# Transposing two bf16 channels as one 4-byte element on VectorE, with TensorE reading the result at a step of 2

## The chip, the cores and the metric

One core of a Trainium2 chip (trn2). The metric is the device time of one execution in microseconds. The four runs of the kernel before agree within 0.2% of their median (244.49 to 245.45 us). All times compared here are of runs taken in the same rounds on the same chip as runs of the kernel before. Times of the profiler's span (243.1 us for the kernel before) are about 1.8 us shorter than the timed ones.

## The reference

Attention in chunks of 64 positions, then a feed-forward with a product of two branches and no other nonlinearity:

```python
# q, k, v: (8, 8, 576, 64) = batch, heads, positions, channels; chunk = 64
scores = q_c @ k_c.T / sqrt(64)              # within each chunk
attn   = softmax(scores)
x      = (attn @ v_c), heads side by side    # (4608, 512)
a, b   = x @ w1, x @ w2                      # 512 -> 1024
out    = ((a * b) @ w3) @ w_out              # 1024 -> 1024 -> 512
```

## The kernel before

The kernel works in bf16 with float32 accumulation. 4608 tokens are handled as 18 pairs of 256 tokens (p = 0 to 17). One string lists every step in program order: `T` transposes q or k, `S` scores, `E` exponential, `P` the product with v, `N` normalises, `X` transposes x, `A`, `B` the products by w1, w2, `C`, `M` make a*b, `V`, `W`, `Z` multiply w3 by w_out once, `O` the output. Lower-case letters are loads.

The kernel transposes on VectorE in blocks of 32 by 32 elements (BL = 32) and arranges channels in such blocks. For pairs 0 to 7 it uses the blocks where they lie; for later pairs a DMA moves blocks between partitions. These are the parts that the change touches (KO = 4, BL = 32, NB = 4, GT = 512, PT = 256, UT = 128, H = 8, CH = 64, FO = 8):

```python
def do_T(p, s, h=None):                  # transpose q (s=0) or k (s=1) of a pair
    g = p // 2
    if g not in qkT_t:
        qkT_t[g] = asb.tile([P, 2, 2, 2, H, CH], bf, tag="qkT", bufs=2, name="qkT")
    inorder(nc.vector.transpose(
        qkT_t[g][:, :, p % 2, s, heads(h)].rearrange("p e h (y t) -> p h t e y", t=2),
        qk_t[p][:, s, heads(h)].rearrange("p h (t e y) -> p h t e y", t=2, e=2)))

# do_S, pairs 0 to 7: two products per block, accumulated
mm(s_t[p][half[i % 2], i // 2, h * CH:(h + 1) * CH],
   lhsT=qkT_t[g][blk[i], e, m, 1, h, :], rhs=qkT_t[g][blk[i], e, m, 0, h, :],
   start=(e == 0), stop=(e == 1))

def do_X(p, u):                          # transpose x
    g, m = divmod(p, 2)
    if p < 8:
        t0 = m * PT + u * UT
        inorder(nc.vector.transpose(
            new_xt(g)[:].rearrange("p (o t) -> p o t", o=KO)[:, :, t0:t0 + UT]
            .rearrange("p o (m y) -> p m o y", y=BL),
            xn_t[p][:, u].rearrange("p r (c n) (z o) -> p (r c) o n z", c=2, o=KO)))
    else: ...                            # the same into xm, which a DMA moves into xt

# do_AB: x is the moving operand of every product by w1 and w2
rhs = new_xt(p // 2)[:].rearrange("p (o t) -> p o t", o=KO)          # p >= 8: "p (s o t) -> p o s t"
for ki in range(KO):
    mm(ps_t[p, j][:, which, i * n:(i + 1) * n],
       lhsT=(w1, w2)[which][:, ki, f * P:(f + 1) * P], rhs=rhs[:, ki],
       start=(ki == 0), stop=(ki == KO - 1))

def do_V(f):                             # transpose a part of w3
    w3T_t[f] = msb.tile([P, FO, P], bf, tag="w3T", bufs=4, name="w3T")
    inorder(nc.vector.transpose(
        w3T_t[f][:].rearrange("p k (f y) -> p f k y", y=BL),
        w3[:, NB * f:NB * (f + 1), :].rearrange("p f (k x) -> p f k x", x=BL)))
```

Products are 256 columns wide for pairs 0 to 3 (256 of them) and 512 wide from pair 4 on (448 of them).

The softmax here doesn't subtract the row's maximum and nothing guards it: scores larger than these inputs give would overflow.

## Time and profile before

| | kernel before |
|---|---|
| time, median | 244.97 us (4 runs, 244.49 to 245.45) |
| span of the profiled run | 243.1 us |
| TensorE busy | 225.9 us, 93% |
| VectorE busy | 153.7 us, 63% |
| TensorE's waits | 7.3 us for the first q, k transposes, then none over 1.4 us |

The page gives each engine's busy time, TensorE's waits by releaser, groups of instructions by line and shape, and the chain of work that ended last. In the chain of waits, "PE ab_ps x64" with its duration is 64 products by w1 and w2. The lines themselves are shown in the prediction.

### The profile page before, as it was taken

What the parts mean: (1) busy time and instruction counts of PE and PEld (TensorE: products, weight loads), DVE (VectorE), ACT (ScalarE), POOL (GpSimd) and SP (SyncE); (2) the same over time, 40 slices, a digit from 0 to 9 for tenths busy, and PEclk for the clock granted to TensorE, in tenths of its full rate; (3) what the DMA queues carried; (4) which work ended last, traced back from release to release, by engine and by line L of the source; (5) the groups of instructions that cost most, each with busy time, mean ns of one, the idle gap of its engine ahead of it and who ended that gap; (6) DMA issues with size and microseconds to landing.
All of it is one profiled execution on the core that took longest, in us unless ns stands there. A gap on an engine that the chain in (4) does not pass through costs nothing.

```text
span 243.1 us, 6347 instructions
## 1 busy us (share of the span) xinstructions
PE 225.9 (93%) x2731; PEld 120.3 (49%) x2753; DVE 153.7 (63%) x232; ACT 85.1 (35%) x116; POOL 83.3 (34%) x112
## 2 busy tenths in 40 slices
PE   1299989999999979999999999999999999999994
PEld 1247868864545444444444444444444444444443
DVE  1856799689899578999998899918440332143000
ACT  2412323423333343534326335162332332332322
POOL 8847974665986444773260240000000000000000
PEclk9999999999999999999999999999999999999999
DMA  7999999999999999999999893735502200400244
GB/s 179 179 185 180 186 168 199 196 193 170 154 172 218 226 228 252 173 219 192 209 237 213 251 137 83 173 89 203 145 0 89 86 0 0 175 0 1 86 173 173
DMA packets 93595, 37.63 MB, mean 155 GB/s; under 512 B 75008, under 2 KB 86528, under 8 KB 93568
## 3 DMA queue, kind: packets, MB, share of 16 engines
q0 software_dynamic: 82592, 18.88, 83.9%
q1 hardware_dynamic: 9936, 17.83, 24.8%
q10 hardware_dynamic: 1040, 0.52, 0.8%
q8 instruction: 21, 0.34, 0.6%
q14 instruction: 6, 0.05, 0.1%
HBM read 38.80 MB, written 9.44 MB: 198 GB/s over the span
## 4 chain that ended last, share of the span: by engine, by line
PE 70%; DMA 16%; DVE 5%; SPq 3%; issue 2%; POOL 2%; ACT 0%; DVEq 0%; POOLq 0%
PE ab_ps L92 38%; PE o_ps L92 23%; PE w_ps L92 6%; DMA w<-in_moe_w_dram 4%; DMA qkm<-qkT 3%; DMA xt<-xm 3%; DMA qk<-in_k_dram 3%; DMA qk<-in_q_dram 3%; SPq L189 3%; PE s_ps L92 2%; PE pv L92 2%; DVE qkT L197 2%; DVE xn L260 1%; DVE ab L341 1%; POOL vbuf L95 1%
## 5 line engine op out<-in xcount | busy, mean ns | idle before, releaser
L92 PE MATMUL ab_ps<-xt,w 128*128 128x512 bf16 (+1 forms) x681 | 126.8, 342 | 1.4 <-DVE xt L272 0.9
L92 PEld LDWEIGHTS <-w 128*128 128x128 bf16 x704 | 67.3, 98 | 55.4 <-DVE xt L272 1.4
L341 DVE TENSOR_TENSOR ab<-a_sb,ab_ps 128x512 bf16<-128x512 f32 x71 | 47.8, 674 | 43.5 <-ACT a_sb L326 43.3
L326 ACT COPY a_sb<-ab_ps 128x512 f32<-128x512 f32 x71 | 41.6, 586 | 81.3 <-PE ab_ps L92 81.1
L92 PE MATMUL o_ps<-w3o,ab 128*128 128x512 bf16 (+1 forms) x285 | 63.3, 373 | 0.6
L197 DVE STREAM_TRANSPOSE qkT<-qk 128x1024 bf16<-128x1024 bf16 x36 | 45.1, 1289 | 8.0 <-ACT qk L140 5.5
L92 PEld LDWEIGHTS <-ab 128*128 128x128 bf16 x296 | 28.5, 98 | 32.3
L95 POOL DMA_DIRECT2D vbuf<-in_v_dram x40 | 33.9, 855 | 17.9 <-DMA qk<-in_k_dram 4.8
L371 ACT COPY o_sb<-o_ps 128x1024 f32<-128x1024 f32 x17 | 17.2, 1012 | 45.2 <-PE o_ps L92 41.3
L260 DVE TENSOR_TENSOR xn<-pv,rc 128x512 bf16<-128x512 f32 x36 | 24.9, 692 | 1.4
L95 POOL DMA_DIRECT2D qk<-in_q_dram x23 | 18.1, 790 | 9.9 <-DMA qk<-in_k_dram 3.1
L95 POOL DMA_DIRECT2D qk<-in_k_dram x23 | 18.0, 785 | 8.8 <-DMA vbuf<-in_v_dram 5.1
L230 ACT ACTIVATE e<-s_ps 128x1024 bf16<-128x1024 f32 x16 | 15.9, 1028 | 2.5 <-PE s_ps L92 2.2
L92 PE MATMUL w_ps<-wo,w3T 128*128 128x512 bf16 x62 | 13.9, 379 | 0.1
L280 DVE STREAM_TRANSPOSE xm<-xn 128x512 bf16<-128x512 bf16 x20 | 13.6, 697 | 0.2
L257 DVE RECIPROCAL rc<-pv 128x8 f32<-128x8 f32 x36 | 6.9, 192 | 9.9 <-PE pv L92 9.9
L95 POOL DMA_DIRECT2D w<-in_moe_w_dram x16 | 11.1, 697 | 5.8 <-DMA vbuf<-in_v_dram 2.3
L92 PEld LDWEIGHTS <-e 64*32 64x32 bf16 (+1 forms) x832 | 7.8, 97 | 8.5 <-issue 7.1
L272 DVE STREAM_TRANSPOSE xt<-xn 128x512 bf16<-128x512 bf16 x16 | 11.4, 711 | 0.5
L92 PE MATMUL pv<-vbuf,e 64*32 64x65 bf16 (+1 forms) x832 | 10.2, 198 | 1.5 <-ACT e L230 1.1
L92 PEld LDWEIGHTS <-qkT 32*64 32x64 bf16 x512 | 5.5, 117 | 11.0 <-DVE qkT L197 7.9
L364 DVE COPY o_sb<-o_ps 128x256 f32<-128x256 f32 x1 | 0.4, 425 | 16.0 <-PE o_ps L92 16.0
(24 smaller groups left out, 52.9 us busy)
## 6 DMA issues: line engine op xcount, KB each, us to landing
out_dram<-o_sb SPq DMA_DIRECT2D x17, 512.0 KB, 3.2
qkm<-qkT SPq DMA_DIRECT2D x40, 128.0 KB, 4.6
vbuf<-in_v_dram POOLq DMA_DIRECT2D x32, 128.0 KB, 8.6
w<-in_moe_w_dram POOLq DMA_DIRECT2D x16, 256.0 KB, 9.6
qk<-in_q_dram POOLq DMA_DIRECT2D x11, 256.0 KB, 6.9
qk<-in_k_dram POOLq DMA_DIRECT2D x11, 256.0 KB, 7.5
xt<-xm SPq DMA_DIRECT2D x40, 64.0 KB, 3.2
wo<-in_moe_w_out_dram POOLq DMA_DIRECT2D x4, 256.0 KB, 8.4
```

The costliest lines, as they stand in the source:

```text
L92: return inorder(nc.tensor.matmul(*a, **kw))
L95: return inorder(nc.gpsimd.dma_start(dst, src))
L189: inorder(nc.sync.dma_start(dst, src))
L197: inorder(nc.vector.transpose(qkT_t[g][:, :, p % 2, s, heads(h)].rearrange("p e h (y t) -> p h t e y", t=2), qk_t[p][:, s, heads(h)].rearr ...
L230: inorder(nc.scalar.activation(e_t[p][:, :, heads(hh)], s_t[p][:].rearrange("p u (h q) -> p u h q", q=CH)[:, :, heads(hh)], Exp, scale=sca ...
L257: inorder(nc.vector.reciprocal(rc[:], pv[:, :, :, D:W]))
L260: inorder(nc.vector.tensor_mul(xn_t[p][:, u], pv[:, :, :, 0:D], rc.to_broadcast([P, 2, 4, D])))
L272: inorder(nc.vector.transpose(new_xt(g)[:].rearrange("p (o t) -> p o t", o=KO)[:, :, t0:t0 + UT] .rearrange("p o (m y) -> p m o y", y=BL), ...
L280: inorder(nc.vector.transpose(xm_t[g][:, u, :, m].rearrange("p o (c y) -> p c o y", y=BL), xn_t[p][:].rearrange("p u r m d -> p (u r) m d" ...
L326: inorder(nc.scalar.copy(a_t[p, j][:], ps_t[p, j][:, 0, :]))
L341: inorder(nc.vector.tensor_mul(o, view(a_t.pop((p, j))[:]), view(ps_t.pop((p, j))[:, 1, :])))
L371: inorder(nc.scalar.copy(o_sb[:], ps_t.pop(p)[:]))
```

## The change

In the profile before, a transpose of 512 elements per partition takes 697 ns and one of 1024 takes 1217 ns, so each further element costs about 1.02 ns. The intent is to halve the elements: two neighbouring bf16 channels are transposed as one 4-byte element. The result has the two channels interleaved, so that TensorE must read one channel at a step of two elements. This is done for q and k of pairs 0 to 7, for x of all pairs, and for w3.

```diff
 # do_T
-            qkT_t[g] = asb.tile([P, 2, 2, 2, H, CH], bf, ...)
+            qkT_t[g] = asb.tile([P, 2, 2, 2, H, CH] if p >= 8 else [P, 2, 2, H, CH, 2], bf, ...)
+        if p < 8:
+            inorder(nc.vector.transpose(
+                qkT_t[g][:, p % 2, s, heads(h)].rearrange("p h y e -> p h (y e)").bitcast(f32)
+                .rearrange("p h (y t) -> p h t y", t=2),
+                qk_t[p][:, s, heads(h)].bitcast(f32).rearrange("p h (t y) -> p h t y", t=2)))
+            return
 # do_S
-   lhsT=qkT_t[g][blk[i], e, m, 1, h, :], rhs=qkT_t[g][blk[i], e, m, 0, h, :],
+   lhsT=qkT_t[g][blk[i], m, 1, h, :, e], rhs=qkT_t[g][blk[i], m, 0, h, :, e],
 # do_X (the branch for p >= 8 likewise)
-                new_xt(g)[:].rearrange("p (o t) -> p o t", o=KO)[:, :, t0:t0 + UT]
+                new_xt(g)[:].bitcast(f32).rearrange("p (o t) -> p o t", o=KO // 2)[:, :, t0:t0 + UT]
                 .rearrange("p o (m y) -> p m o y", y=BL),
-                xn_t[p][:, u].rearrange("p r (c n) (z o) -> p (r c) o n z", c=2, o=KO)))
+                xn_t[p][:, u].bitcast(f32).rearrange("p r (c n) (z o) -> p (r c) o n z", c=2, o=KO // 2)))
 # do_AB
-            rhs = new_xt(p // 2)[:].rearrange("p (s o t) -> p o s t", s=2, o=KO)
+            rhs = new_xt(p // 2)[:].rearrange("p (s a t b) -> p a b s t", s=2, a=KO // 2, b=2)
-            rhs = new_xt(p // 2)[:].rearrange("p (o t) -> p o t", o=KO)
+            rhs = new_xt(p // 2)[:].rearrange("p (a t b) -> p a b t", a=KO // 2, b=2)
-                   lhsT=(w1, w2)[which][:, ki, f * P:(f + 1) * P], rhs=rhs[:, ki],
+                   lhsT=(w1, w2)[which][:, ki, f * P:(f + 1) * P], rhs=rhs[:, ki // 2, ki % 2],
 # do_V, do_W: w3T becomes [P, FO // 2, P, 2], written as f32, read as lhsT=w3T[:, ki // 2, :, ki % 2]
 # load_wo: rows of w_out in the matching order, two at a time (half the packets)
 # ... cut
```

More of the change, by code (lines that the diff above doesn't have):

```diff
@@ L177, in load_wo @@
         for i in range(NB):
-            load(wo[i * BL:(i + 1) * BL],
-                 moe_w_out[i * DF // NB:(i + 1) * DF // NB].rearrange("(k x) n -> x k n", x=BL))
+            load(wo[i * BL:(i + 1) * BL].rearrange("p (k e) n -> p k (e n)", e=2),
+                 moe_w_out[i * DF // NB:(i + 1) * DF // NB].rearrange("(k x e) n -> x k (e n)", x=BL, e=2))
     half = [slice(0, CH), slice(CH, P)]
@@ L195, in do_T @@
         if g not in qkT_t:
-            qkT_t[g] = asb.tile([P, 2, 2, 2, H, CH], bf, tag="qkT", bufs=2, name="qkT")
+            qkT_t[g] = asb.tile([P, 2, 2, 2, H, CH] if p >= 8 else [P, 2, 2, H, CH, 2], bf,
+                                tag="qkT", bufs=2, name="qkT")
+        if p < 8:
[4 more added lines that the diff above has]
+            return
         inorder(nc.vector.transpose(
@@ L272, in do_X @@
             inorder(nc.vector.transpose(
-                new_xt(g)[:].rearrange("p (o t) -> p o t", o=KO)[:, :, t0:t0 + UT]
+                new_xt(g)[:].bitcast(f32).rearrange("p (o t) -> p o t", o=KO // 2)[:, :, t0:t0 + UT]
                 .rearrange("p o (m y) -> p m o y", y=BL),
-                xn_t[p][:, u].rearrange("p r (c n) (z o) -> p (r c) o n z", c=2, o=KO)))
+                xn_t[p][:, u].bitcast(f32).rearrange("p r (c n) (z o) -> p (r c) o n z", c=2, o=KO // 2)))
         else:
             if g not in xm_t:
-                xm_t[g] = asb.tile([P, 2, KO, 2, UT], bf, tag="xm", bufs=2, name="xm")
+                xm_t[g] = asb.tile([P, 2, KO // 2, 2, 2 * UT], bf, tag="xm", bufs=2, name="xm")
             inorder(nc.vector.transpose(
-                xm_t[g][:, u, :, m].rearrange("p o (c y) -> p c o y", y=BL),
-                xn_t[p][:].rearrange("p u r m d -> p (u r) m d")[:, :, 2 * u:2 * u + 2]
-                .rearrange("p c n (z o) -> p c o n z", o=KO)))
+                xm_t[g][:, u, :, m].bitcast(f32).rearrange("p o (c y) -> p c o y", y=BL),
+                xn_t[p][:].bitcast(f32).rearrange("p u r m d -> p (u r) m d")[:, :, 2 * u:2 * u + 2]
+                .rearrange("p c n (z o) -> p c o n z", o=KO // 2)))
     def do_H(g, a):
@@ L303, in do_AB @@
         if p >= 8:
-            rhs = new_xt(p // 2)[:].rearrange("p (s o t) -> p o s t", s=2, o=KO)
+            rhs = new_xt(p // 2)[:].rearrange("p (s a t b) -> p a b s t", s=2, a=KO // 2, b=2)
         else:
-            rhs = new_xt(p // 2)[:].rearrange("p (o t) -> p o t", o=KO)
+            rhs = new_xt(p // 2)[:].rearrange("p (a t b) -> p a b t", a=KO // 2, b=2)
             if p < 4:
-                rhs = rhs[:, :, p % 2 * PT:(p % 2 + 1) * PT]
+                rhs = rhs[:, :, :, p % 2 * PT:(p % 2 + 1) * PT]
         fs = (f,) if p >= 4 else (2 * j, 2 * j + 1)
@@ L380, in do_V @@
     def do_V(f):
-        w3T_t[f] = msb.tile([P, FO, P], bf, tag="w3T", bufs=4, name="w3T")
+        w3T_t[f] = msb.tile([P, FO // 2, P, 2], bf, tag="w3T", bufs=4, name="w3T")
         inorder(nc.vector.transpose(
-            w3T_t[f][:].rearrange("p k (f y) -> p f k y", y=BL),
-            w3[:, NB * f:NB * (f + 1), :].rearrange("p f (k x) -> p f k x", x=BL)))
+            w3T_t[f][:].rearrange("p k y e -> p k (y e)").bitcast(f32).rearrange("p k (f y) -> p f k y", y=BL),
+            w3[:, NB * f:NB * (f + 1), :].bitcast(f32).rearrange("p f (k x) -> p f k x", x=BL)))
     def do_W(m):
@@ L390, in do_W @@
             for ki in range(FO):
-                mm(ps_t["w", m][:, i, :], lhsT=w3T[:, ki, :], rhs=wo[:, ki, :],
+                mm(ps_t["w", m][:, i, :], lhsT=w3T[:, ki // 2, :, ki % 2], rhs=wo[:, ki, :],
                    start=(ki == 0), stop=(ki == FO - 1))
```

## The prediction

> **What bounds the kernel now.** I read the busy times first, then TensorE's waits, then the busy times by stretch, the groups by shape, and last the timeline and the chain of waits over the first 40 us.
>
> The page's busy line, the summary of TensorE's waits, and one run of products from the chain of waits:
>
> ```profile
> PE 225.9 (93%) x2731; PEld 120.3 (49%) x2753; DVE 153.7 (63%) x232; ACT 85.1 (35%) x116; POOL 83.3 (34%) x112
> ...
> PE z_ps L92 <- DVE qkT L197: 7.3, 1, 7.3
> PE s_ps L92 <- issue: 1.4, 1, 1.4
> PE z_ps L92 <- DVE zero L110: 1.2, 1, 1.2
> PE pv L92 <- ACT e L230: 1.1, 1, 1.1
> PE ab_ps L92 <- DVE xt L272: 0.9, 2, 0.6
> ...
> 208.78 13.81 PE ab_ps L92 x64
> ```
>
> TensorE is busy for 225.9 of 243.1 us. A busy TensorE need not be at its peak, so I checked the rate: 13.81 us for 64 products of 512 columns is 215.8 ns each. Its work counted up: 448 + 64 + 280 products of 512 columns (x by w1 and w2 from pair 4 on; w3 by w_out; the output) at 215.8 ns make 170.9 us, 256 of 256 columns at 114.7 ns (32 in 3.67 us on the timeline) make 29.4, the last output's 16 half-wide ones about 1.8, scores and PV of 18 pairs at about 0.65 us each some 23.5. That is 225.6, so nearly all of the busy time is work at full rate. Only the idle 17.2 us can be won without making TensorE's work itself cheaper, and this change does not. Of that, 3.2 us lie after the last product, 1.2 before the first; the waits above show where the rest is. VectorE is the cause of two entries, 7.3 and 0.9 us.
>
> Busy times by stretch show that VectorE's load elsewhere costs nothing:
>
> ```profile
> 50.00:60.00 10.00, 9.95 (x56) 5.34 (x55) 10.00 (x11) 3.20 (x4) 5.63 (x8) 1.00 1.81 181
> 120.00:130.00 10.00, 9.95 (x77) 4.73 (x78) 9.90 (x15) 3.79 (x5) 3.69 (x5) 1.00 1.26 219
> ```
>
> Columns after the width: TensorE, weight load, VectorE, ScalarE, GpSimd. VectorE is full in both stretches and TensorE is busy for 9.95 of 10 us all the same: the order is tuned so that VectorE works ahead.
>
> The groups by shape, for the sizes (busy us, mean ns):
>
> ```profile
> L197 DVE STREAM_TRANSPOSE qkT<-qk 128x1024 bf16<-128x1024 bf16 x36 | 45.1, 1289 | 8.0 <-ACT qk L140 5.5 <-DMA qk<-in_q_dram 1.3 <-PE s_ps L92 0.9
> L280 DVE STREAM_TRANSPOSE xm<-xn 128x512 bf16<-128x512 bf16 x20 | 13.6, 697 | 0.2
> L272 DVE STREAM_TRANSPOSE xt<-xn 128x512 bf16<-128x512 bf16 x16 | 11.4, 711 | 0.5
> L382 DVE STREAM_TRANSPOSE w3T<-w 128x1024 bf16<-128x1024 bf16 x8 | 9.4, 1217 | 1.7 <-DMA w<-in_moe_w_dram 1.7
> ```
>
> 512 and 1024 elements take 697 and 1217 ns: 520/512 = 1.016 ns per element and 177 ns fixed.
>
> The two places where VectorE delays TensorE, on the timeline, and the piece of the chain of waits before the second:
>
> ```profile
> 5.93 1.99 ACT L140 CAST qk<-raw 128x1024 bf16<-128x1024 f32 x2 [3.39 <-DMA raw<-in_q_dram]
> 7.00 5.33 DVE L197 STREAM_TRANSPOSE qkT<-qk 128x1024 bf16<-128x1024 bf16 x4 [5.46 <-ACT qk L140]
> 9.54 1.07 PE L92 MATMUL z_ps<-qkT 32*64 32x64 bf16 x64 [7.31 <-DVE qkT L197]
> ...
> 24.09 3.67 PE L92 MATMUL ab_ps<-xt,w 128*128 128x256 bf16 x32 [0.33 <-DVE xt L272]
> ...
> 35.48 1.92 PE L92 MATMUL ab_ps<-xt,w 128*128 128x256 bf16 x16 [0.55 <-DVE xt L272]
> ...
> 23.61 6.76 DMA qk<-in_q_dram
> 30.38 0.02 issue
> 30.40 1.32 DVE qkT L197
> ```
>
> The first scores wait for two transposes in a row. The product at 35.48 us waits for a chain that starts with q of pair 3 landing at 30.38: one q transpose, one product ab, then twice (rc, xn, xt).
>
> [...] The changed q, k transpose writes 4-byte elements at a step of two words[...]. The trace speaks neither way: in the x transpose each bf16 read is 8 bytes from the last and still runs at 697 to 711 ns, but that is a read. [...] No operand of TensorE in the kernel before has a step[...]. [...]
>
> **The change part by part.** The order of instructions is the same on every engine; only shapes change.
>
> 1. q, k of pairs 0 to 7: 16 transposes from 1024 bf16 to 512 4-byte elements. 177 + 512 x 1.016 = 697, plus about 40 for the stepped write (1289 against 1217 before shows 72 for twice the elements): about 740 ns instead of 1289. 16 x 0.55 = 8.8 us off VectorE.
> 2. x: 36 transposes from 512 to 256 elements, 177 + 260 = about 437 instead of 697 to 711. 36 x 0.265 = 9.5 us off.
> 3. w3: 8 from 1217 to about 697, 4.2 us off.
> 4. w_out lands in rows twice as long: half the packets for 1 MB, a small relief for the DMA.
> 5. TensorE: the same products, moving x at a step of 2, scores with both operands at a step of 2, w3's weights at a step of 2. I take 0 for this.
>
> So VectorE falls by 22.5 us, from 153.7 to about 131. On the path that sets the end there is far less. At the start: the second cast ends at 7.92 us, so the second transpose ends near 8.7, not 9.5, and the first scores start about 0.8 us earlier. The following wait is unchanged, since the exponential follows the scores. But this gain is provisional: weights arrive in step with the DMA (99% busy from the second slice to the 24th), and products up to 35 us cannot run ahead of them. The chain that ends at 35.48 is fixed at its start by the landing at 30.38. It shortens by one q transpose (1.32 to 0.74: 0.58) and two x transposes (0.27 each: 0.54), in all 1.1 us, so X's end moves from 35.43 to about 34.3. TensorE, which was ready at 34.93, would be ready at about 34.0 to 34.5 with the earlier gain partly stopped by weights. So the product at 35.48 starts near 34.4: 1.1 us won. From there to the end TensorE runs almost without a wait, and the 1.1 us is carried; I take 0.1 off for waits that reappear. 245.2 - 1.0 = 244.2 us.
>
> **The rivals.** (a) The stepped read slows TensorE. Then the loss is large: if each 512-wide product took 1.1 times as long, 448 x 21.6 ns = 9.7 us, and if twice, 97 us and more. If only the scores' weight loads took twice as long, 8 pairs x up to 0.6 us, some 4 us. For it: nothing in the trace has such a read. [...] I give 15% to a loss over 2%. (b) The q, k transpose doesn't reach 740 ns because of its stepped write[...]. 35% likely, and hardly visible in the time. (c) The gain is absorbed: the DMA is full until 140 us, and TensorE may meet a load that it now outruns. For it: q of pair 3 and w3's first half (VectorE waits 1.7 us for it at 49.6). Against: the first product by w3 starts at 51.7, with the transpose done at 50.9, and would now be done at 50.3. This gives 245.0. (d) The wait named issue (1.4 us in the scores at 87 us), for which the profile shows no releaser, goes or comes again elsewhere: 1.4 us either way. (e) VectorE was the bound of the middle and 10 us come free: excluded by TensorE's 9.95 of 10 us in its fullest stretches.
>
> **Range and chances.** Free steps give 243.0 to 245.3, with (d) 246. 8 in 10: 242.8 to 246.0. Over 2% faster means under 240.3, and would need 5 us of idle time where VectorE causes 8.2, most of it the start's loads and casts: 3%. Within 2%: 82%. Slower by over 2%: 15%, all of it (a).
>
> **What would show it.** Right: VectorE's busy time near 131 us, TensorE's still near 226; the x transposes at 437 ns, w3's at 697, q and k at 740[...]; the first scores at 8.7 us; the wait for xt in front of the third pair's products at 34.3 to 34.5 us; 64 products by w1, w2 still in 13.8 us. Wrong: 64 products in 15 us or more, or 64 scores in over 0.7 us (rival a); a new TensorE wait on a DMA (rival c); 4-byte transposes as long as before, with which the time would not change at all.

The forecast's sum: 245.2 us (the profiled run), less the 1.1 of the start, plus the 0.1 for waits that reappear, 244.2 us. What stands for the 4-byte transposes is an estimate from the 1.016 ns per element of bf16, and the 0 for the stepped reads was the author's estimate; the trace before had neither such a transpose nor such a read. "Full rate" is 215.8 ns per product of 512 columns.

## The result, and the profile after

| | before | after |
|---|---|---|
| time, median | 244.97 us (244.49 to 245.45) | 248.66 us (248.28 to 249.66) |
| ratio | | 1.0157 (95%: 1.012 to 1.0194) |
| span of the profiled run | 243.1 | 247.9 |
| TensorE busy | 225.9 | 230.7 |
| VectorE busy | 153.7 | 132.5 |

A ratio here is always the mean time of one kernel's runs over that of the other's of the same rounds, so not quite the ratio of the medians beside it. The change made the kernel 1.6% slower. The profiled run is the slowest of the four (249.66 us), so its spans overstate the loss by about 1 us; durations of single instructions don't suffer from this.

The busy line and the summary of TensorE's waits, after:

```profile
PE 230.7 (93%) x2731; PEld 118.9 (48%) x2753; DVE 132.5 (53%) x232; ACT 85.1 (34%) x116; POOL 83.2 (34%) x112
...
PE z_ps L92 <- DVE qkT L201: 6.7, 1, 6.7
PE ab_ps L92 <- DMA w<-in_moe_w_dram: 1.3, 2, 0.9
PE s_ps L92 <- issue: 1.2, 1, 1.2
```

VectorE lost 21 us of work, as intended. TensorE gained 4.8 us of busy time with the same instructions (its products by w1 and w2 alone gained 5.5, from 126.8 to 132.3 us on the two pages). So the loss is not a wait: TensorE itself has become slower. The groups by shape show that the transposes did what they were meant to do (busy us, mean ns):

```profile
L201 DVE STREAM_TRANSPOSE qkT<-qk 128x512 f32<-128x512 f32 x16 | 10.9, 697 | 10.8 <-ACT qk L140 5.9 <-DMA qk<-in_q_dram 3.7 <-DMA qk<-in_k_dram 1.2
L290 DVE STREAM_TRANSPOSE xm<-xn 128x256 f32<-128x256 f32 x20 | 8.2, 431 | 0.2
L282 DVE STREAM_TRANSPOSE xt<-xn 128x256 f32<-128x256 f32 x16 | 7.1, 445 | 0.5
L392 DVE STREAM_TRANSPOSE w3T<-w 128x512 f32<-128x512 f32 x8 | 5.7, 707 | 4.4 <-PE w_ps L92 2.3 <-DMA w<-in_moe_w_dram 2.0
```

The last lines of the chain of waits (start us, us, what) show where the time came from:

```profile
191.41 14.50 PE ab_ps L92 x64
...
206.18 6.64 PE o_ps L92 x30
212.82 14.50 PE ab_ps L92 x64
```

64 products by w1 and w2 took 13.81 us before and take 14.50 us now: 226.6 ns each in place of 215.8. The output products between them, which read nothing at a step, still take 6.64 us for 30. The other engines do the same work in this stretch as before (VectorE 4.8 us, ScalarE 5.1, and the DMA moves about 40 GB/s in both), so heavier traffic of theirs is not the reason. The trace's start-to-start times say the same of every stage: 226 to 227 ns at 512 columns wherever x is read, 113.3 in place of 109.2 at 256 columns, and under 1 ns between the even and the odd channel. 448 x 10.8 ns = 4.84 us, and 256 x 4.1 ns = 1.05 us, 5.9 in all. On the two timelines the wide products begin 0.1 us late (82.94 against 82.82) and have ended 4.7 us late (227.16 against 222.43): 4.6 us, and the wait named "issue" among them is 0.2 us shorter than before, so the 4.8 us are there.

The timeline of the first 40 us shows what became of the gain there (TensorE alone):

```profile
26.70 0.71 PE L92 MATMUL s_ps<-qkT 32*64 32x64 bf16 x64
27.81 1.08 PE L92 MATMUL ab_ps<-xt,w 128*128 128x256 bf16 x8 [0.40 <-DMA w<-in_moe_w_dram]
29.80 1.08 PE L92 MATMUL ab_ps<-xt,w 128*128 128x256 bf16 x8 [0.91 <-DMA w<-in_moe_w_dram]
30.81 0.70 PE L92 MATMUL pv<-vbuf,e 64*32 64x65 bf16 x64
31.44 5.62 PE L92 MATMUL ab_ps<-xt,w 128*128 128x256 bf16 x48
```

The first scores started at 8.90 us (9.54 before) and the scores above at 26.70 (27.68 before). Then TensorE had outrun the last quarter of w1 and w2, and waited for it. Behind that wait, 48 products run without a break, where before the third pair's had waited 0.55 us for x. The first product by w3 starts at 51.81 us, 51.70 before: nothing was left of the gain.

### The profile page after: what moved, and what is told of

Same layout as the page of the kernel before. It is cut to its first block, busy times and chain, and to the rows that moved or that the text cites. A ratio compares the mean times of both kernels' runs of the same rounds, so it can differ in the third digit from the quotient of the medians.

```text
span 247.9 us, 6347 instructions
## 1 busy us (share of the span) xinstructions
PE 230.7 (93%) x2731; PEld 118.9 (48%) x2753; DVE 132.5 (53%) x232; ACT 85.1 (34%) x116; POOL 83.2 (34%) x112
## 4 chain that ended last, share of the span: by engine, by line
PE 82%; DMA 11%; SPq 2%; issue 2%; POOL 1%; ACT 1%; DVE 0%; DVEq 0%; POOLq 0%
PE ab_ps L92 46%; PE o_ps L92 25%; DMA w<-in_moe_w_dram 7%; PE w_ps L92 6%; DMA qk<-in_k_dram 3%; PE pv L92 3%; PE s_ps L92 2%; SPq L189 2%; DMA qkm<-qkT 1%; POOL vbuf L95 1%; ACT e L239 0%; POOL qk L95 0%; POOL w L95 0%; ACT a_sb L336 0%; DVE o_sb L374 0%
## 5 line engine op out<-in xcount | busy, mean ns | idle before, releaser
L92 PE MATMUL ab_ps<-xt,w 128*128 128x512 bf16 (+1 forms) x681 | 132.3, 348 | 1.9 <-DMA w<-in_moe_w_dram 1.3
L92 PEld LDWEIGHTS <-w 128*128 128x128 bf16 x704 | 66.0, 96 | 62.7 <-DMA w<-in_moe_w_dram 1.7
L351 DVE TENSOR_TENSOR ab<-a_sb,ab_ps 128x512 bf16<-128x512 f32 x71 | 48.3, 680 | 56.4 <-ACT a_sb L336 56.2
L206 DVE STREAM_TRANSPOSE qkT<-qk 128x1024 bf16<-128x1024 bf16 x20 | 25.1, 1296 | 0.9 <-PE s_ps L92 0.8
L201 DVE STREAM_TRANSPOSE qkT<-qk 128x512 f32<-128x512 f32 x16 | 10.9, 697 | 10.8 <-ACT qk L140 5.9
L92 PEld LDWEIGHTS <-w3T 128*128 128x128 bf16 x64 | 6.3, 98 | 7.3
```

The lines of the kernel that those rows point to most:

```text
L92: return inorder(nc.tensor.matmul(*a, **kw))
L201: inorder(nc.vector.transpose(qkT_t[g][:, p % 2, s, heads(h)].rearrange("p h y e -> p h (y e)").bitcast(f32) .rearrange("p h (y t) -> p h ...
L206: inorder(nc.vector.transpose(qkT_t[g][:, :, p % 2, s, heads(h)].rearrange("p e h (y t) -> p h t e y", t=2), qk_t[p][:, s, heads(h)].rearr ...
L351: inorder(nc.vector.tensor_mul(o, view(a_t.pop((p, j))[:]), view(ps_t.pop((p, j))[:, 1, :])))
```

## The experiments

Theory A: reading x as the moving operand at a step of 2 makes each product slower, and nothing else in the change costs anything. Rivals: the loss sits in another part (B), or the 4-byte transposes or VectorE's new rhythm slow TensorE's reads (C). Ten kernels ran.

| run | time, median | before in the same rounds | ratio (95%) |
|---|---|---|---|
| x undone | 243.93 | 244.92 | 0.9958 (0.9934 to 0.9983) |
| changed, x read contiguously | 244.75 | 244.92 | 1.0003 (0.9974 to 1.0031) |
| before, x read at a step of 2 | 251.63 | 244.92 | 1.0287 (1.0255 to 1.0318) |
| q, k only | 243.88 | 244.85 | 0.9953 (0.9927 to 0.9978) |
| w3 only | 244.93 | 244.85 | 0.9999 (0.9973 to 1.0025) |
| x undone, two moves | 242.89 | 244.85 | 0.9918 (0.9894 to 0.9942) |
| changed, contiguous from pair 4 | 244.50 | 244.83 | 0.9966 (0.9927 to 1.0006) |
| before, step of 2 from pair 4 | 248.97 | 244.83 | 1.0164 (1.0126 to 1.0202) |

The two scans of patterns ran once each, for their traces, so their state is unknown and their total times are not used.

### The x part undone

```diff
 # on the changed kernel: do_X and rhs of do_AB as before
-                new_xt(g)[:].bitcast(f32).rearrange("p (o t) -> p o t", o=KO // 2)[:, :, t0:t0 + UT]
+                new_xt(g)[:].rearrange("p (o t) -> p o t", o=KO)[:, :, t0:t0 + UT]
 # ... cut
-                   ... rhs=rhs[:, ki // 2, ki % 2],
+                   ... rhs=rhs[:, ki],
```

> The changed kernel with the x part undone (x transposed as bf16, read contiguously); q, k, w3 and w_out stay as changed. Theory A (the read of x at a step of 2 slows each product, 215.8 to 226.6 ns at 512 columns, 109.2 to 113.3 at 256, and nothing else in the change costs): products back at 215.8 and 109.2 ns, and the gain of the start remains, so 0.2 to 1.2 us faster than the kernel before, about 244.3. Rival B (the loss sits in the scores, the w3 products, or the loads that now come in another rhythm): still at or above 246.

Measured: correct, 0.42% faster than the kernel before, products of 512 columns back at 215.8 ns and of 256 at 109.2. From the chain of waits:

```profile
187.31 13.81 PE ab_ps L92 x64
...
208.03 13.81 PE ab_ps L92 x64
```

The scores and w3's products still read at a step of 2, and cost nothing. So the x part is worth about 4.7 us (248.66 against 243.93, of two sets of rounds), and Rival B is out.

### The changed kernel with x read contiguously, and the kernel before with x read at a step of 2

```diff
 # on the changed kernel (wrong channels):
+        elif p >= 4:
+            rhs = new_xt(p // 2)[:].rearrange("p (o t) -> p o t", o=KO)
 # on the kernel before (wrong channels):
+        elif p >= 4:
+            rhs = new_xt(p // 2)[:].rearrange("p (a t b) -> p a b t", a=KO // 2, b=2)
 # ... cut: p >= 8 likewise; p < 4 by another pattern
```

> Wrong result on purpose: the changed kernel in full, 4-byte transposes included, but products read x contiguously (wrong channels). Theory A (the read): products at 215.8 ns and a time of 243.3 to 244.5. Rival C (the products are slow because of where or how the 4-byte transposes write, or because VectorE's new rhythm meets TensorE's reads): products stay at 226 ns, the time at 248.

> Wrong result on purpose: the kernel before, all transposes in bf16, with one thing changed: products read x at a step of 2. Theory A: products at 226.6 (512 columns) and 113.3 ns (256 columns), so 448 x 10.8 + 256 x 4.1 = 5.9 us more than before, less what of it falls into waits of the first 35 us: 249.5 to 251. Rival C: products at 215.8, time as before.

Measured: by the product, both came out as Theory A has it: 215.8 ns with 4-byte transposes and contiguous reads, 226 to 227 ns with bf16 transposes and reads at a step of 2. The read alone decides. The last 64 products by w1 and w2 in the chains of waits, first of the changed kernel with contiguous reads, then of the kernel before with stepped ones:

```profile
209.24 13.81 PE ab_ps L92 x64
```

```profile
214.62 14.50 PE ab_ps L92 x64
```

By the total, both missed: 244.75 (expected up to 244.5) and 251.63 (expected up to 251). A look at the waits showed a flaw of the test. In the wrong-valued reads of pairs 0 to 3, products of pair 0 waited for x of pair 1, a wait that neither original has in its program. The second kernel's waits:

```profile
PE z_ps L92 <- DVE qkT L197: 7.5, 1, 7.5
PE ab_ps L92 <- DVE xt L272: 3.4, 5, 1.4
```

3.4 us in place of 0.9 is more than the excess of 0.6 needs (one profile each). So I ran both again with pairs 0 to 3 left alone.

### The same two, from pair 4 on only

```diff
 # on the changed kernel, after its own rhs (wrong channels):
+        if p >= 8:
+            rhs = new_xt(p // 2)[:].rearrange("p (s a b t) -> p a b s t", s=2, a=KO // 2, b=2)
+        elif p >= 4:
+            rhs = new_xt(p // 2)[:].rearrange("p (a b t) -> p a b t", a=KO // 2, b=2)
 # on the kernel before: "p (s a t b) -> p a b s t" and "p (a t b) -> p a b t" for the same pairs
```

> Wrong result on purpose, and a cleaner form of the run in which the changed kernel read x contiguously: there the first products waited for x of the next pair, which neither kernel does. Here pairs 0 to 3 read as in the changed kernel and only the 448 products of 512 columns from pair 4 on read contiguously. Theory A: 448 x 10.8 ns = 4.8 us under the changed kernel's 248.7, about 243.8 (243.3 to 244.5); 512-column products at 215.8, 256-column ones at 113.3 ns. Rival C (the 4-byte transposes themselves cost): above 246.

> Wrong result on purpose: the kernel before, with only the 448 products of 512 columns from pair 4 on reading x at a step of 2. Theory A: 4.8 us over before, 249.2 to 250.0, products at 226.6 ns, everything else as before. Rival C: as before, 244.9.

Measured: 244.50 and 248.97 us. The pattern of waits in the program was the same as the originals', and the products took 215.8 and 226.6 ns as expected. The read of the 448 wide products is worth 4.1 to 4.2 us by both (248.97 - 244.83, and 248.66 - 244.50 of two sets of rounds), not quite the 4.8 of the products' sum; the second total missed its range by 0.2 us. In the two profiles the wait named "issue" in the scores at 87 us was 1.4 us in the kernel before and 0.4 in this one. In these profiles that closes the account: from the start of the wide products to their end the stepped kernel lost 3.7 us (82.80 to 226.09, against 82.82 to 222.43), and with the 1.0 us that its wait was shorter, 4.7. Single profiles don't show that this holds for the timed runs. For those the rest of about 0.7 us stays open.

### How the cost follows the pattern

```diff
 # on the kernel before: the last four pair groups read x in other patterns (wrong values)
+        step = {10: 2, 12: 3, 14: 4, 16: 8}.get(p, 1)                     # first scan
+        v = new_xt(p // 2)[:, 0:n0 * step].rearrange("p (t s) -> p s t", s=step)[:, 0:m, 0:512 // m]
+        v = {10: "(t s e) -> s t e", s=2, e=8; 12: "(t s e)", s=4, e=2;    # second scan, abridged
+             14: "(t s) -> s t", s=16, 4 rows; 16: x[:, 1:513]}
```

> Wrong result on purpose: the kernel before, but the 64 products of each of the last four pair groups read x at a step of 2, 3, 4 and 8 elements in turn. Theory D ([...]512 columns at a step of 2 span 2048 bytes in 226.6 ns, 9.0 bytes per ns): 227, 340, 453 and 906 ns each. Theory E (any non-contiguous pattern loses a fixed 5%): about 227 ns at every step. [...]

> Wrong result on purpose: the kernel before, but the products of the last four pair groups read x in four patterns of 512 elements: runs of 8 elements at a pitch of 16; runs of 2 at a pitch of 8; single elements at a step of 16; contiguous but one element off. Theory D1 (the cost is 1.77 ns for each 16-byte line touched, at least 215.8 ns in all): 64 lines 216, 256 lines 453, 512 lines 900, 65 lines 216 ns. Theory D2 (the cost follows the bytes spanned, 9.0 per ns): 227, 453, 1810, 216 ns.

The chain of waits of the first scan, steps of 3, 4 and 8:

```profile
167.23 21.86 PE ab_ps L92 x64
...
196.00 28.94 PE ab_ps L92 x64
...
231.84 57.60 PE ab_ps L92 x64
```

The timeline of the second scan: runs of 2 at a pitch of 8, single elements at a step of 16, and contiguous but one element off (63 records of 64):

```profile
166.40 29.10 PE L92 MATMUL ab_ps<-xt,w 128*128 128x512 bf16 x64
...
202.25 58.90 PE L92 MATMUL ab_ps<-xt,w 128*128 128x512 bf16 x64
...
269.09 14.03 PE L92 MATMUL ab_ps<-xt,w 128*128 128x512 bf16 x63
```

A timeline's duration includes the end of the last product; the table takes start-to-start times within a stretch. Lines are a unit of counting: the stretches of 16 bytes that one product's read enters in a partition, counted again each time it comes back. The tile of x holds only 4096 bytes per partition, so the step of 8 walks it in two passes and the step of 16 in four: their 512 entries fall on 256 and 128 different lines.

| pattern of 512 elements | bytes walked | lines entered | ns per product | ns per line |
|---|---|---|---|---|
| contiguous | 1024 | 64 | 215.8 | (3.4) |
| contiguous, one element off | 1024 | 65 | 216.7 | (3.3) |
| runs of 8 at a pitch of 16 | 2048 | 64 | 216 | (3.4) |
| step of 2 | 2048 | 128 | 226.6 | 1.77 |
| step of 3 | 3072 | 192 | 340 | 1.77 |
| step of 4 | 4096 | 256 | 452 | 1.77 |
| runs of 2 at a pitch of 8 | 4096 | 256 | 452 | 1.77 |
| step of 8 | 8192 | 512 | 900 | 1.76 |
| step of 16 | 16384 | 512 | 918 | 1.79 |

All nine fit one rule: a product takes the larger of its contiguous time (215.8 ns here) and about 1.77 ns for each 16-byte line that it enters. The worst fit is the step of 16, 918 ns where the rule gives 906, 1.3% more. The 1.77 comes from the step of 2; the other rows test it, all in bf16. 256 columns at a step of 2 enter 64 lines, 113.3 ns, and were measured at 113.3. That 16 bytes are the stretch to count by is seen in two pairs of rows. By stretches of 8 bytes the step of 4 would enter 512 and the runs of 2 only 256, yet both took 452 ns; by 32 bytes the step of 8 would enter 256 and the step of 16 512, yet they took 900 and 918. The fixed 5% (Theory E) falls with the step of 3; the rule by bytes walked (Theory D2) falls with the runs of 8 and with the step of 16, where it wanted 227 and 1810 ns.

A rival for the last two rows is the clock: the granted clock of TensorE, as the profile gives it, had a mean of 0.55 in the products at a step of 8, and in the second scan of 0.80 from 188 to 217 us and 0.66 from 224 to 282, two stretches that the step of 16 shares with other products. But at 0.55 a step of 8 took 1.76 ns per line, and at 1.00 steps of 3 and 4 took 1.77, so the lower clock is not seen in the step of 8. For the step of 16 (1.79) no stretch at 1.00 is there to compare.

By this fit a step of 2 lies just past the edge. Contiguous products leave 215.8 ns for their 64 lines, which would do for 215.8 / 1.77 = 122. A step of 2 needs 128.

### q and k only, w3 only

```diff
 # on the kernel before: do_T and do_S as changed, nothing else
 # on the kernel before: do_V, do_W and load_wo as changed, nothing else
```

> The kernel before with only the q, k part of the change (pairs 0 to 7 transposed as 4-byte elements, scores read at a step of 2). Theory A2 (all the gain of the version with x undone comes from the q, k transposes of the first 35 us): 243.7 to 244.4, about 0.9 us under before; 64 scores still in 0.64 us. Rival G (w3 or the longer rows of w_out give the gain): the time of before, 244.9.

> The kernel before with only the w3 part (4-byte transposes of w3, weights loaded at a step of 2, w_out in rows twice as long). Theory A2: nothing, 244.5 to 245.2, since w3's 8 transposes end ahead of their products anyway; w3 products at 215.8 ns. Rival G: about 244.

Measured: q and k alone give 0.47%, about 1.0 us, and w3 gives nothing (0.9999). Both as Theory A2 had it (in the profile before, w3's first transpose ends at 50.88 us, the first product by w3 starts at 51.70, and TensorE waits for none of the eight). Part of the gain is seen at the start: in the profile of q and k alone the first scores start at 8.75 us in place of 9.54, and the first product by w3 at 51.00 in place of 51.70, 0.7 us earlier. After it, the wait named "issue" at 87 us is 0.5 us in place of 1.4. In the profile of the version with x undone only 0.25 us are left at the first product by w3 (51.45), and that wait is again 0.5. These waits change from run to run, so how much of the timed 1.0 us the start gives is not shown.

### The x part undone, and two moves in the order

```diff
-i2 q2 k2 v2 i3 q3
+i2 q2 k2 i3 v2 q3
-A0.3 E2 T3.0 B0.3 ... A1.3 X2.1 B1.3
+A0.3 E2 B0.3 ... A1.3 X2.1 T3.0 B1.3
```

> The version with x undone (q, k, w3 as changed), with two moves in the order: the last quarter of w1, w2 is loaded ahead of v of pair 2, and the q transpose of pair 3 stands behind pair 2's x transposes instead of ahead of them. Theory H (what stops the start's gain is the wait for these weights, 0.8 and 0.3 us at 27 to 30 us, and then the chain hanging on q of pair 3): another 0.5 to 1.0 us, 242.9 to 243.4. Rival: v of pair 2 or w3 now comes too late, and the wait moves there: 243.9 or more.

Measured: correct, 242.89 us, 0.82% faster than the kernel before and the best of all. (The upper 95% bound of the ratio, 0.9942, and the lower one of the version without the moves, 0.9934, just overlap; the medians, from different chips, differ by 1.04 us. In the same rounds on the same chip ran q and k alone, 243.28 to 244.44; the six runs here lie at 242.62 to 243.40, and the medians differ by 0.99 us.) TensorE on the timeline, the same stretch as shown for the changed kernel:

```profile
27.54 1.92 PE L92 MATMUL ab_ps<-xt,w 128*128 128x256 bf16 x16
29.39 0.70 PE L92 MATMUL pv<-vbuf,e 64*32 64x65 bf16 x64
30.02 3.67 PE L92 MATMUL ab_ps<-xt,w 128*128 128x256 bf16 x32
34.01 1.92 PE L92 MATMUL ab_ps<-xt,w 128*128 128x256 bf16 x16 [0.32 <-DVE xt L282]
```

The wait for the last weights is gone, and the third pair's products start at 34.01 us. The first product by w3 starts at 50.32 us, 1.4 us ahead of the kernel before. So the wait for w1 and w2 was part of what stopped the start's gain. Both moves were made at once; what each gave is not shown, and some of the total may again be the "issue" wait at 87 us, which this profile doesn't have.

## Why the prediction was wrong, point by point

The predicted time was 244.2 us with a range of 242.8 to 246.0; measured were 248.66.

- **The step that failed is item 5 of the change, "I take 0 for this".** Reading x at a step of 2 costs 10.8 ns for each product of 512 columns and 4.1 for each of 256, 5.9 us by their sum, of which about 4.7 show in the time. The 0 was the author's estimate, with no such read in the trace before. By the fit to the scans, at 1.77 ns per line, the 215.8 ns of a 512-column product leave time for 122 lines, and a step of 2 needs 128, 5% too many.
- **The rival was named, its size was not.** Rival (a) gave 9.7 us at 1.1 times and 97 at twice; the truth is 1.05 times. The chances left almost nothing between 246.0 us and a loss of 2%, which is where the loss fell. The other two stepped reads in item 5 are indeed free: 64 scores still take 0.64 us in the chain of waits, and w3's products 10.74 us for 49, before and after.
- **The transposes came out within 2% of what was worked out, or better.** x at 431 to 445 ns (437 predicted), w3 at 707 (697), q and k at 697 (740). Rival (b), a slow stepped write, is out. VectorE ended at 132.5 us (131).
- **The start's 1.1 us was right in its cause and too large for this kernel.** The first scores came at 8.90 us (8.7 predicted), the third pair's products at 35.08 (34.4); their x was ready at 34.85 (34.3). The prediction said the gain might be "partly stopped by weights"; it was, by 1.3 us of waits for w1 and w2. With x undone, about 1.0 us is left in the time, as with q and k alone. The chain through q of pair 3, on which the prediction built, was only part of the reason: pulling these weights forward and q out of the way, both at once, gave another microsecond.
- **That VectorE's 21 us would not come through was right.** No stage is seen to gain from them after the start: in the profile with x undone the lead over the kernel before stays at 0.25 us from the first product by w3 to 86 us, and after the "issue" wait at 87 us it does not grow. The x part is nearly half of them (9.7 us). With x's reads contiguous from pair 4 on, the changed kernel is no faster (244.50) than with the x part undone (243.93), but it still reads pairs 0 to 3 at a step of 2, so the gain of x's shorter transposes alone was not measured cleanly.
- **The count of TensorE's work agreed partly by luck.** The 114.7 ns for a product of 256 columns include the end of the last product on the timeline; their starts lie 109.2 ns apart. And 23.5 us for scores and PV is too much: from pair 8 on, two pairs share one 0.64 us stretch of scores, and PV takes 0.38 us a pair in place of 0.63. The count left out the products on zeros at the start, about 4 us. The rate of 215.8 ns, on which the argument rests, was read rightly. The page also gives the DMA 90% or more of the time in most of the slices named, and 80 to 90% in one, not 99%.

## What to carry to other kernels

An engine that isn't the bound can be relieved at the cost of the one that is (here VectorE by 21.2 us of busy time, TensorE 4.8 us more): before handing TensorE a new access pattern for the moving operand, count the 16-byte lines per product and compare with the time of the product, here 1.77 ns per line against 215.8 ns at 512 columns. In this kernel stepped reads cost nothing in w3's products (10.74 us for 49, before and after) and in the scores (0.64 us for 64), and 10.8 ns each in the products by w1 and w2 that fill the time. And a gain at the start of this kernel held only as far as the next load (1.3 us of waits for w1 and w2): look at which transfer the faster engine will run into, and move that one too.

## What the traces show of the hardware

- TensorE's moving operand at 512 columns of bf16: a step of 2 costs 5% (226.6 against 215.8 ns), 3 costs 1.6 times (340), 4 costs 2.1 times (452) and 8 costs 4.2 times (900). A step of 8 bytes took 452 ns, of 16 bytes 900, and of 32 bytes hardly more (918).
- Contiguous products in a stream start every 215.8 ns at 512 columns and every 109.2 at 256. The other bound is 1.77 ns per 16-byte line entered: 226.6 ns for the 128 lines of a step of 2.
- Transposes of 4-byte elements on VectorE: 512 of them take 697 to 707 ns and 256 take 431 to 445, about the rate of bf16 per element (697 to 711 ns for 512). The one that writes at a step of two 4-byte words is no slower (697 ns).
- In the first scan the products at a step of 8 followed each other without a gap, and the mean granted clock of that stretch was 0.55, against 1.00 at a step of 4. Why it was lower is not shown. The columns of the two lines are as in the prediction (granted clock third from the end):

```profile
196.00:224.70 28.70, 28.70 (x64) 7.32 (x63) 4.81 (x7) 5.11 (x8) 0.00 (x0) 1.00 0.05 19
231.80:289.00 57.20, 57.20 (x65) 7.88 (x63) 4.80 (x7) 5.11 (x8) 0.00 (x0) 0.55 0.03 10
```

- TensorE's waits that the profile puts down to "issue" take 0.2 to 1.4 us and change from run to run. In the kernels before and after, the longest (1.4 and 1.2 us) stands in both behind the 1372nd weight load; the next stands behind the 479th before (0.4 us) and behind the 224th after (0.8). (The shorter ones at 12 to 16 us fall where the trace lacks some records of matmuls.) What they wait for is not shown.
